# Fourier mixing with a soft mixture of experts: two tiles Z for the turned spectra, and their moves spread over each batch

## The chip, the core and the metric

The kernel runs on one core of a Trainium2 chip. Its engines are called as in the profile: PE (TensorE, matmuls), DVE (VectorE), ACT (ScalarE), POOL (GpSimd) and SP (SyncE, which here issues nearly all DMA transfers). The metric is the time of one execution on the device in microseconds (us), the median of three runs. Lower is better.

## The reference

Eight batches of 2496 tokens with 256 channels go through a Fourier transform along the tokens, a complex linear layer with soft shrinkage, and the transform back; the result is the input of a soft mixture of 8 experts with 4 slots each. Cut to what matters:

```python
X = np.fft.rfft(x, axis=1)                     # x: (8, 2496, 256)
Yr = Xr @ w_r - Xi @ w_i + b_r
Yi = Xr @ w_i + Xi @ w_r + b_i
Y  = sign(Yr) * max(|Yr| - 0.01, 0) + 1j * (the same of Yi)
y  = np.fft.irfft(Y, n=2496, axis=1)           # the tokens of the mixture, N = 19968

logits     = y @ phi                           # (N, 32)
d          = softmax of logits over the tokens
slot_input = d.T @ y                           # (32, 256)
slot_out   = relu(slot_input @ w1[e]) @ w2[e]  # for each expert e and its 4 slots
c          = softmax of logits over the slots
out        = c @ slot_out                      # (N, 256)
```

## The kernel before

The length 2496 is split as 39 x 64, so the transform is done in two steps of small matmuls. The main work runs over 40 steps: 8 batches of 5 groups of 4 frequencies out of 39 (`steps`, line 1071). For each step the program does, by the names that the profile shows:

- `pa`: the first transform (39) of a later batch, on PE; its result goes by way of `ast` to DRAM (`adr`) and comes back turned as `ap`.
- `px`: the second transform (64), on PE from `ap`; ACT, DVE and POOL split its result into high and low parts `xth`, `xtl`, `xsm`, `xsh`, `xsl`.
- `pk` and `py`: the linear layer, on PE from those parts; DVE adds them up to `ut`, and the shrinkage makes `rt` of `ut`, by turns on POOL and on ACT with DVE.
- `tp_p`: the projection on phi. `c_stages`: once a batch, the logits of the batch before go back to tokens. Their coefficients leave for DRAM and come back turned (`gd` written from `g_sb`, then read as `gp`), go through matmuls (`pL`), a maximum (`mx`, transposed on PE as `pm`), exponentials, a second such way through DRAM (`ed`, `eb`), and end as weights `dd` with which `pr` sums up the slots.

`pr` needs the spectra turned, with frequencies on the partitions. For groups 3 and 4 of a batch (and all of the last batch) PE transposes them into tiles `T`. For groups 0 to 2 of batches 0 to 6 (`moved`, line 578) DVE transposes blocks of 32 x 32 into one tile `Z` for each batch (line 669, in the trace `z<-rt`), and sixteen transfers of 96 KB each move these blocks to their partitions in a tile `Y` (`z_move`, line 583, in the trace `y<-z`). There is one tile Z and there are two tiles Y (line 276). A new Z can be written only when all sixteen moves out of the old one have landed.

Order and queues: every operation is a generator step with a due time on a common plan clock, 4 units a step, 20 a batch (a batch takes some 51 us in the trace). A heap hands the steps out in the order of their times, and what is handed out stays in that order on its engine. So an engine, and SP too, does its instructions one behind the other, and one that waits holds up those behind it. SP's transfers take eight semaphores in turn, so a transfer also waits until the eighth before it has landed. `PLAN["zd"]` has the due times of the sixteen moves within their batch: three at 14.9 to 15.9, thirteen at 21.2 to 26.6; in batch 6 the last six come at 28.7 to 30.2 (`z6`).

In the tail the experts' weights are loaded, 32 pieces of 512 KB (`load_w`, line 1116; `wl` lists the due time, the place and the layer of each, counted from the end of the main work, TB = 166). They go to tiles that are free by then: place 't' takes a tile of the pool `ta`, which is opened where the tiles of the first transform lay (`nw`: 13 tiles of 4 KB a partition), 'Y' and 'Z' a third of a tile Y or Z, others what their letters say. The same pool then serves the last stage (`ct`, `chl`: the turned combination weights). From the third group of batch 7 on, the spectra `rt` lie in parts of a tile Z as well (line 648). `hps` is the first product of the experts, `po` the second, `pq` in the last stage the output blocks, written from `ost`.

Of the kernel before, what the change touches and what calls it, by code (L numbers as in the profile page):

```python
# [17 lines left out]
B, N, D = 8, 2496, 256  # L18
N1, N2 = 39, 64
R, G = 3, 22  # L20
# [59 lines left out]
def _constants():  # L80
# [84 lines left out]
PLAN = {  # L165
    "aq": [-10.6, -6.6, -2.6, 1.4, 5.4, 7.4],
    "aqo": [0.4, 0.5],
    "aqt": ["pf", "pt"],
    "eo": {0: [3.95, 1.95], 4: [3.95, 3.9], 5: [2.05, 2.0]},
    "xq": 7.5,  # L170
    "aq2": {(2, 0): [6.6, 8.8, 9.2, 10.4], (2, 1): [8.8, 11.2, 11.6, 13.4]},
    "th": 'PA',
    "sh": 'A',
# [18 lines left out]
    "to": 0.4,  # L192
    "ws": [-29, -28.9, -28.8, 2],
    "late": {'6': {'cms': [13.1, 13.2, 18, 22.65, 22.66, 22.67], 'pd': [16.681, 16.6], 'pdt': ('pl', 'pl'), 'pda': 1, 'pLt': ('ps', 'ps'), 'pr': [17.15, 18.3, 20.179, 19.707, 19.902], 'pL': [6.6, 7.3], 'pm': 8.51, 'pmr': 9.35, 'pb': 10.36, 'pe': [11.747, 11.96, 12.419], 'pg': [0.875, 1.275], 'fr': {'sinv': 0, 'm2': 0, 'f1': 0, 'suni': 0}, 'pbx': 1.2, 'pet': ('pf', 'pf'), 'so': 0.2}, '5': {'so': 1.5}, '4': {}},
    "T_": {'wl': [[-31, 't', 1], [-30, 't', 1], [-29, 't', 1], [-21.8, 't', 2], [-20.6, 't', 2], [-16.9, 't', 1], [-16.8, 't', 1], [-16.6, 't', 2], [-16.1, 't', 2], [-15.6, 't', 2], [-15.1, 't', 2], [-14.6, 't', 2], [-14.1, 't', 2], [-13.6, 'Y', 1], [-13.1, 'Y', 1], [-12.4, 'c', 2], [-11.8, 's', 1], [-11.2, 'a', 1], [-10.6, 'a', 1], [-10, 'a', 1], [-9.5, 'Ww_r', 1], [-8.7, 'Wnws', 1], [-8.6, 'Wwd', 1], [0.01, 'k', 1], [0.01, 'u', 1], [0.02, 'x', 2], [0.02, 'x', 2], [0.02, 'x', 2], [1.4, 'R', 2], [1.4, 'R', 2], [1.73, 'Z', 2], [1.74, 'Z', 2]], 'cl': 2.0, 'cp': 46.5, 'ct': 46.6, 'du': [[2.55, 2]], 'd1': [], 'cm': [19.9, 19.91, 19.92, 25, 25.1, 25.2], 'cm7': [0.71, 1.7, 1.95, 2.7, 2.71, 2.8], 'ye': 0.2, 'te': [[5.6, 0.2], [5.5, 0.4]], 'pg': [-15.49, -11.49, -7.99, -3.934, -2.9], 'yt': 0.578, 'wr': -30.6, 'tp': [0, 0.6, 0.85, 0.5], 'tt': [0.4, 0.55, 0.821, 1.25, 0.994], 'z': 1.686, 'th': [0.1, 0.12], 'tl': [0.24, 0.25], 'pgt': ['ps', 'ps', 'ps', 'pf', 'pf'], 'ch': [0.263, 0.5, 0.7, 1.0, 1.514, 2.0], 'te7': 'AAAAAAAAAA', 'op': 2, 'ot': [3, 5, 7], 'gt': [-14.5, -10.5, -7.0, -3.93, -2.89]},
    "f1": [-1.6, -1.5],
    "kw": [[-28.6, 4], [-28.4, 12]],
    "ap1": 1.85,
    "f0": 0.2,
    "nw": [13, 9],  # L200
    "te": 'A',
    "tp": [0.5, 0.9, 1.9, 1.8],
    "tt": [0.52, 2.505],
# [22 lines left out]
    "hA": 3,  # L226
    "tlr": 1.85,
    "xle": 0.45,
# [32 lines left out]
def fourier_soft_moe_kernel(ctx: ExitStack, tc: tile.TileContext, t: dict, out: bass.AP):  # L261
# [11 lines left out]
    psum_bufs = {"pf": 2, "pl": 2, "pt": 2, "ps": 1, "pr": 1}  # L273
    a_bufs = {"xr": 3, "xh": 3, "xl": 3, "ast": 3}
    main_bufs = {"xsm": 2, "k1": 2, "ut": 2, "rt": 4, "lg": 2}
    chain_bufs = {"ap": 3, "xth": 3, "xtl": 3, "xsh": 3, "xsl": 3, "Z": 1, "Y": 2, "T": 8, "p_sb": 2, "g_sb": 1,
                  "gp": 2, "L": 1, "ee": 1, "g7": 1, "dd": 2, "mx": 1, "dg": 1, "cm": 1, "cs": 1, "ch": 2, "cl": 2,
                  "cb": 1}

# [3 lines left out]
    def wtile(shape, dt, tag, name):  # L283
        if tag in a_bufs:
            return wap.tile(list(shape), dt, tag=tag, name=name, bufs=a_bufs[tag])
        if tag in main_bufs:
            return wmp.tile(list(shape), dt, tag=tag, name=name, bufs=main_bufs[tag])
        return wcp.tile(list(shape), dt, tag=tag, name=name, bufs=chain_bufs[tag])

    parts = {}  # L290

    def part(tag, n, name):

        z, o = parts.get(tag, (None, 12))
        if o + n > 12:
            z, o = wtile([128, 12 * 256], F32, tag, name), 0
        parts[tag] = (z, o + n)
        return z[:, o * 256 : (o + n) * 256]

    x = t["x"]  # L300
# [24 lines left out]
    def sp(**kw):  # L325
        with tc.issue_after(sp_last[-1].ins) if sp_last else nullcontext():
            sp_last.append(tc.keep_in_program_order(nc.sync.dma_start(**kw)))
# [36 lines left out]
    def load_x0():  # L364
        g = GP * len(x0)
        xr = (part("Y", 2, f"x0_{g}") if g >= 8 * GP else wtile([128, GP * D], F32, "T", f"x0_{g}")).rearrange("p (g d) -> p g d", d=D)
        sp(out=xr, in_=x[0, :, g : g + GP, :])
        x0.append(xr[:P1])
# [10 lines left out]
    while len(x0) < G // GP:  # L379
# [6 lines left out]
        wmp.tile([128, n, 64], F32, tag=f"smov{i}", name=f"smov{i}") for i, n in enumerate((KG + 1, K1 + 1 - KG))  # L386
    ]
    wri = part("Z", 4, "wri").rearrange("p (g d) -> p g d", d=D)
    pk0, pk1 = (cons.tile([128, sum(w)], F32, tag=n, name=n) for n, w in PACK.items())
    cols = {}  # L390
    for z, (n, w) in zip((pk0, pk1), PACK.items()):
        o = 0
# [29 lines left out]
    def a_unit(b, g, u):  # L422
# [19 lines left out]
        if g == gs[0]:  # L442
            own = PLAN["ast4"].get((b, g))
            if own == "Z":
                asts[(b, g)] = part("Z", 4, f"ast{b}_{g}")[:QA].rearrange("p (g d) -> p g d", d=D)
            elif own:
                asts[(b, g)] = wtile([QA, 4, D], F32, own, f"ast{b}_{g}")
            else:
                asts[(b, g)] = wtile([QA, 6, D], F32, "ast", f"ast{b}_{g}")
# [132 lines left out]

    def z_move(b):
        for n, (i, j) in enumerate(itertools.product(range(4), range(4))):
            yield 20 * b + (PLAN["zd"][n] if b < B - 2 or n < 10 else PLAN["z6"] + 0.3 * (n - 10))
            if n == 0:
                parts.pop("Y", None)
                yts[b] = wtile([128, 4, 2, KZ, 32], F32, "Y", f"y{b}")
            sp(
                out=yts[b][32 * j : 32 * j + 32, i].rearrange("p h k x -> p (h k x)"),  # L590
                in_=zts[b][32 * i : 32 * i + 32, j].rearrange("p h k x -> p (h k x)"),
            )
# [523 lines left out]
    def load_w(loc, layer):  # L1116
        i = len(wbuf)
        w, h, e = wlist[layer].pop(0)
        if w == 0:
            src = t["moe_w1"][e, h * 128 : h * 128 + 128, :]  # L1120
        else:
            src = t["moe_w2"][e, h * 512 : h * 512 + 512, :].rearrange("(p f) d -> p (f d)", f=4)
        if loc in "YZT":
            parts = [part(loc, 4, f"w{i}")]
        elif loc == "c":
            parts = [wtile([128, F // 4], F32, z, f"w{i}_{z}{q}") for z in ("ch", "cl") for q in range(2)]
        elif loc == "h":
            parts = [wtile([128, F // 4], F32, z, f"w{i}_{z}{q}") for z in ("xsh", "xsl") for q in range(2)]
        elif loc == "a":
            parts = [wtile([128, F], F32, "ap", f"w{i}")]  # L1130
        elif loc == "t":
            parts = [ta_tile(f"w{i}")]
        elif loc == "s":
            parts = [wmp.tile([128, K1 + 1 - KG, 64], F32, tag="smov1", name=f"w{i}").rearrange("p m q -> p (m q)")[:, :F]]
        elif loc[0] == "W":
            parts = [wmp.tile([128, F // 2], F32, tag=loc[1:] + z, name=f"w{i}_{z}") for z in "hl"]
        else:
            tags = {"x": ("xth", "xtl"), "k": ("k1", "k1"), "u": ("ut", "ut"), "R": ("rt", "rt")}[loc]
            parts = [wtile([128, F // 2], F32, tags[q], f"w{i}_{q}") for q in range(2)]
        n = F // len(parts)  # L1140
        for q, r in enumerate(parts):
            sp(out=r, in_=src[:, q * n : q * n + n])
        wbuf[(w, h, e)] = parts
# [4 lines left out]
    def ta_tile(name):  # L1148
        return pools["ta"].tile([128, F], F32, tag="tw", name=name, bufs=NTA)
# [36 lines left out]
    for b in range(B - 1):  # L1186
        step_to(z_move(b))
# [8 lines left out]
    for t_ in PLAN["T_"]["wl"]:  # L1196
        at(t_[0], load_w, *t_[1:])
    at(PLAN["T_"]["z"], slot_stationary)
    T_ = PLAN["T_"]
# [325 lines left out]
```

## Time and profile before

| what | value |
|---|---|
| time, median of 3 runs | 526.41 us (525.14 to 527.59) |
| the profiled execution | 527.98 us, of which the span of its instructions is 526.2 us |
| PE busy | 484.4 us, 92% |
| DVE, ACT, POOL busy | 363.3 us (69%), 319.8 us (61%), 271.0 us (52%) |
| DMA | 131.04 MB, mean 249 GB/s |
| chain of work that ended last | PE 72%, DMA 10%, DVE 8%, issue 3%, POOL 3%, ACT 2% |

The span runs from the first to the last instruction; the profiled execution's time has 1.8 us around it. In the rows of a timeline, the number in square brackets is how long the engine was idle before the instruction, and what by the trace ended that wait; where an instruction waits for several things, this is the one that came last by the profile. Rows of SP are the issue of transfers, not their landing; a row's "x4" is four instructions, and its duration runs from the start of the first to the end of the last.

### The profile page before, as it was taken

How to read it: one execution, taken by the hardware profiler on the slowest of the kernel's cores; microseconds unless marked ns; L12 is line 12 of the kernel's file. 1: busy time of each engine (PE TensorE's matmuls, PEld its weight loads, DVE VectorE, ACT ScalarE, POOL GpSimd, SP SyncE). 2: the span in 40 equal slices, each digit the busy share in tenths (PEclk: the TensorE clock that was granted, in tenths of full speed). 3: DMA queues.
4: the chain of work that ended last, by engine and by line, in shares of the span. 5: the costliest groups of instructions: out<-in, count | busy, mean ns of one | idle time of the engine just before them, and what ended most of it. 6: DMA issues, size and time to landing. Idle time of an engine off the chain costs nothing.

```text
span 526.2 us, 11975 instructions
## 1 busy us (share of the span) xinstructions
PE 484.4 (92%) x4438; PEld 394.7 (75%) x4438; DVE 363.3 (69%) x718; ACT 319.8 (61%) x724; POOL 271.0 (52%) x277
## 2 busy tenths in 40 slices
PE   8889999999979998999899989998997389999991
PEld 4479788878868887888789778888986376468880
DVE  3255975798759966986799589959874186446671
ACT  4357566677656766676577667755754156247771
POOL 0026667767846785678567766844460213214210
PEclk9989999999999999999999999999999599999997
DMA  8998688686877697779677967766586979359998
GB/s 288 323 292 294 218 283 231 191 279 189 253 212 248 174 263 212 243 197 293 185 262 198 287 202 242 189 190 193 173 228 182 355 276 308 110 164 385 405 405 338
DMA packets 90461, 131.04 MB, mean 249 GB/s; under 512 B 40204, under 2 KB 61836, under 8 KB 90404
## 3 DMA queue, kind: packets, MB, share of 16 engines
q1 hardware_dynamic: 89460, 128.16, 75.9%
q10 hardware_dynamic: 944, 2.13, 1.2%
q8 instruction: 35, 0.57, 0.5%
q14 instruction: 22, 0.18, 0.1%
HBM read 69.25 MB, written 50.00 MB: 227 GB/s over the span
## 4 chain that ended last, share of the span: by engine, by line
PE 72%; DMA 10%; DVE 8%; issue 3%; POOL 3%; ACT 2%; SPq 1%; DVEq 0%; ACTq 0%; POOLq 0%
PE py L333 17%; PE px L333 11%; PE pq L333 10%; PE pa L333 8%; PE pk L333 8%; PE pt L708 3%; PE pr L333 3%; DMA w<-in_moe_w 2%; DMA gd<-g_sb 2%; DVE z L257 2%; PE pc L708 2%; PE pe L333 2%; PE pL L333 1%; PE pd L333 1%; DMA xr<-in_x 1%
## 5 line engine op out<-in xcount | busy, mean ns | idle before, releaser
L257 POOL TENSOR_TENSOR xsl<-xsm,xsh 128x256 fp32r<-128x256 f32 x77 | 70.2, 912 | 117.2 <-ACT xsh L257 116.5
L333 PEld LDWEIGHTS px<-smov,ap 128*128 128x128 f32 x640 | 79.8, 194 | 21.4 <-ACT xsh L257 16.1
L333 PE MATMUL px<-smov,ap 128*128 128x128 f32 x640 | 86.2, 279 | 8.9 <-DVE xtl L257 7.8
L257 DVE SCALAR_TENSOR_TENSOR ut<-py,pk,k 128x256 f32<-128x256 f32 x160 | 69.7, 477 | 23.8 <-PE py L333 21.6
L257 ACT COPY ast<-pa 128x512 f32<-128x512 f32 (+1 forms) x88 | 45.5, 560 | 28.5 <-PE pa L333 28.3
L333 PE MATMUL pk<-xsl,w_rh 128*128 128x256 f32 (+1 forms) x160 | 45.4, 283 | 11.6 <-POOL xsl L257 11.6
L257 DVE TENSOR_TENSOR xtl<-px,xth 128x512 fp32r<-128x512 f32 x80 | 54.3, 680 | 0.1
L257 ACT CAST xsh<-xsm 128x256 fp32r<-128x256 f32 x80 | 32.8, 410 | 35.0 <-DVE xsm L257 34.9
L333 PE MATMUL py<-xth,nwsh 128*128 128x256 f32 (+1 forms) x160 | 53.2, 333 | 0.0
L257 ACT CAST xth<-px 128x512 fp32r<-128x512 f32 x80 | 47.2, 591 | 6.1 <-PE py L333 5.1
L257 POOL TENSOR_TENSOR rt<-ut,rt 128x512 f32<-128x512 f32 x36 | 50.8, 1410 | 0.1
L257 DVE TENSOR_TENSOR xsm<-px,xsm 128x256 f32<-128x256 f32 x80 | 33.3, 416 | 23.2 <-ACT xth L257 17.7
L333 PE MATMUL pk<-xsh,w_rh 128*128 128x256 f32 (+1 forms) x160 | 47.9, 299 | 0.0
L257 ACT COPY xsm<-px 128x256 f32<-128x256 f32 x80 | 30.0, 375 | 27.6 <-PE px L333 23.8
L333 PE MATMUL py<-xth,wdh 128*128 128x256 f32 (+1 forms) x160 | 45.2, 283 | 0.0
L333 PE MATMUL py<-xtl,nwsh 128*128 128x256 f32 (+1 forms) x160 | 45.1, 282 | 0.0
L333 PE MATMUL py<-xth,nwsl 128*128 128x256 f32 (+1 forms) x160 | 45.1, 282 | 0.0
L333 PE MATMUL pk<-xsh,w_rl 128*128 128x256 f32 (+1 forms) x160 | 45.0, 281 | 0.0
L333 PE MATMUL py<-xtl,wdh 128*128 128x256 f32 (+1 forms) x160 | 44.9, 281 | 0.0
L333 PE MATMUL py<-xth,wdl 128*128 128x256 f32 (+1 forms) x160 | 44.9, 280 | 0.0
L257 DVE STREAM_TRANSPOSE z<-rt 128x512 f32<-128x512 f32 x42 | 28.2, 694 | 24.1 <-DMA ap<-adr 10.4
L257 DVE SCALAR_TENSOR_TENSOR rt<-ut,rt 128x512 f32<-128x512 f32 x44 | 37.3, 848 | 9.4 <-ACT rt L257 9.4
(227 smaller groups left out, 1304.2 us busy)
## 6 DMA issues: line engine op xcount, KB each, us to landing
ap<-adr SPq DMA_DIRECT2D x76, 256.0 KB
out<-ost SPq DMA_DIRECT2D x37, 512.0 KB
xr<-in_x SPq DMA_DIRECT2D x35, 512.0 KB
adr<-ast SPq DMA_DIRECT2D x20, 768.0 KB
y<-z SPq DMA_DIRECT2D x112, 96.0 KB
w<-in_moe_w SPq DMA_DIRECT2D x21, 512.0 KB
adr<-ast SPq DMA_DIRECT2D x7, 512.0 KB
w<-in_moe_w SPq DMA_DIRECT2D x14, 256.0 KB
```

The costliest lines, as they stand in the source:

```text
L257: return lambda *a, **k: self.tc.keep_in_program_order(f(*a, **k))
L333: tc.keep_in_program_order(nc.tensor.matmul(**kw))
L708: tc.keep_in_program_order(nc.tensor.transpose(out=out, in_=in_, identity=identity))
```

## The change

There are two tiles Z. The sixteen moves of a batch are spaced evenly: every 1.2 plan units from 15.0 to 33.0 of their batch, in batch 6 every 0.6 units from 15.0 to 24.0. To make room, the pool `ta` has ten tiles in place of thirteen; three of the weights get the new place 'z', the thirds of a tile Z of their own (the key "zw" keeps it apart from the Z that `rt` takes parts of). In `wl` the weights at -21.8 and -20.6 are now of the first layer and those at -16.9 and -16.8 of the second; the ones at -14.8 (before -15.1), -14.6 and -14.1 go to 'z'. The line of `wl` itself is left out below.

```diff
-    "nw": [13, 9],
+    "nw": [10, 9],
...
-    "zd": [14.9, 15.4, 15.9, 21.2, 21.65, 22.1, 22.55, 23.0, 23.45, 23.9, 24.35, 24.8, 25.25, 25.7, 26.15, 26.6],
+    "zd": [15.0, 1.2, 0.6],
     "nd": 4,
-    "z6": 28.7,
...
-    chain_bufs = {"ap": 3, "xth": 3, "xtl": 3, "xsh": 3, "xsl": 3, "Z": 1, "Y": 2, "T": 8, "p_sb": 2, "g_sb": 1,
+    chain_bufs = {"ap": 3, "xth": 3, "xtl": 3, "xsh": 3, "xsl": 3, "Z": 2, "Y": 2, "T": 8, "p_sb": 2, "g_sb": 1,
...
-    def part(tag, n, name):
+    def part(tag, n, name, key=None):
 
-        z, o = parts.get(tag, (None, 12))
+        key = key or tag
+        z, o = parts.get(key, (None, 12))
         if o + n > 12:
             z, o = wtile([128, 12 * 256], F32, tag, name), 0
-        parts[tag] = (z, o + n)
+        parts[key] = (z, o + n)
         return z[:, o * 256 : (o + n) * 256]
...
         for n, (i, j) in enumerate(itertools.product(range(4), range(4))):
-            yield 20 * b + (PLAN["zd"][n] if b < B - 2 or n < 10 else PLAN["z6"] + 0.3 * (n - 10))
+            yield 20 * b + PLAN["zd"][0] + PLAN["zd"][1 + b // (B - 2)] * n
...
         if loc in "YZT":
             parts = [part(loc, 4, f"w{i}")]
+        elif loc == "z":
+            parts = [part("Z", 4, f"w{i}", "zw")]
```

The two tiles are taken in turn. Batches 1, 3 and 5 lie in one and 0, 2, 4 and 6 in the other; `rt` of batch 7, asked for next, gets the tile that batch 5 had, the three weights behind it get batch 6's. On PE, DVE, ACT and POOL the instructions stand in the order in which they stood before; only SP's order differs.

First place: SP around the way through `gd`, in batch 2 (the same pattern stands in every batch). `y` from `z` are the moves of batch 2, `c_dr` stores combination weights, `xr` is input, `adr` from `ast` the first transform's result, `ap` its reading back. Before:

```order
L327 DMA c_dr_126<-cb_2491 128x704
L327 DMA y_2297<-z_2030 32x768 x4
L327 DMA xr_4_2722<-in_x 128x1024
L327 DMA y_2297<-z_2030 32x768
L327 DMA adr_1770<-ast_12_2561 128x1536
L327 DMA y_2297<-z_2030 32x768
L327 DMA ap_4_2783<-adr_1029 64x4x256 x2
L327 DMA gd_2858<-g_sb_2735 64x20x32 x2
L327 DMA gp_2883<-gd_2858 40x704 x2
```

and in the changed kernel:

```order
L327 DMA c_dr_126<-cb_2493 128x704
L327 DMA y_2302<-z_2025 32x768 x2
L327 DMA xr_4_2718<-in_x 128x1024
L327 DMA adr_1771<-ast_12_2562 128x1536
L327 DMA ap_4_2777<-adr_1030 64x4x256 x2
L327 DMA y_2302<-z_2025 32x768 x2
L327 DMA gd_2854<-g_sb_2731 64x20x32 x2
L327 DMA gp_2879<-gd_2854 40x704 x2
```

Of the six moves ahead of `gd` two are left ahead of `xr`, and two stand directly ahead of `gd`; four more of the batch's moves stand behind `gp`.

Second place: SP at the end of the main work, behind the last way through `gd` (batch 6). `w` are the weights, `y` from `z` the last moves of batch 6. Before:

```order
L327 DMA gp_5913<-gd_5903 40x640
L327 DMA y_5443<-z_5201 32x768 x2
L327 DMA w_5956<-in_moe_w 128x1024
L327 DMA w_5963<-in_moe_w 128x1024
L327 DMA y_5443<-z_5201 32x768
L327 DMA w_5966<-in_moe_w 128x1024
L327 DMA y_5443<-z_5201 32x768
L327 DMA w_5973<-in_moe_w 128x1024
L327 DMA y_5443<-z_5201 32x768 x2
L327 DMA w_5989<-in_moe_w 128x1024
```

and in the changed kernel, from the last move of batch 6 on:

```order
L327 DMA y_5448<-z_5196 32x768
L327 DMA c_dr_130<-cb_5630 128x704
L327 DMA w_5766<-in_moe_w 128x1024
L327 DMA w_5825<-in_moe_w 128x1024
L327 DMA ap_4_5859<-adr_4156 64x4x256 x2
L327 DMA gd_5909<-g_sb_5841 64x20x32 x2
L327 DMA gp_5919<-gd_5909 40x704 x2
L327 DMA gp_5919<-gd_5909 40x640
L327 DMA w_5960<-in_moe_w 128x1024
L327 DMA w_5967<-in_moe_w 128x1024
L327 DMA w_5969<-in_moe_w 128x1024
```

The six moves that stood among the weights are gone from there; the last move of batch 6 stands ahead of `c_dr` and of the way through `gd`.

## Rows read from the trace of the kernel before

**Rows 1.** The page, part 1: busy time of PE, share of the span, instructions

```profile
PE 484.4 (92%) x4438; PEld 394.7 (75%) x4438; DVE 363.3 (69%) x718; ACT 319.8 (61%) x724; POOL 271.0 (52%) x277
```

**Rows 2.** Stages: length, busy of PE, PEld, DVE, ACT, POOL; clock, DMA share, GB/s

```profile
150.00:201.00 51.00, 48.90 (x484) 41.18 (x484) 40.42 (x80) 34.70 (x79) 35.41 (x34) 1.00 0.75 227
...
404.00:421.00 17.00, 5.59 (x25) 4.67 (x24) 2.56 (x4) 2.77 (x7) 3.72 (x4) 0.60 1.00 341
421.00:452.00 31.00, 29.05 (x404) 21.95 (x403) 22.24 (x55) 17.41 (x45) 7.13 (x10) 1.00 0.82 287
...
415.80:420.00 4.20, 4.19 (x16) 3.69 (x17) 0.51 (x1) 1.25 (x3) 2.07 (x2) 0.50 1.02 407
```

**Rows 3.** Timeline of PE: start, length, instruction, [idle before, what ended it]

```profile
112.50 0.32 PE L831 MATMUL pm<-pk,mx 117*128 117x117 f32 x1 [0.46 <-DVE mx L257]
...
152.07 1.13 PE L333 MATMUL px<-smov,ap 128*128 128x128 f32 x8 [3.13 <-DVE xtl L257]
...
203.20 1.02 PE L333 MATMUL px<-smov,ap 128*128 128x128 f32 x7 [1.83 <-DVE xtl L257]
...
253.91 0.80 PE L333 MATMUL px<-smov,ap 128*128 128x128 f32 x5 [1.43 <-DVE xtl L257]
...
304.59 0.79 PE L333 MATMUL px<-smov,ap 128*128 128x128 f32 x5 [1.38 <-DVE xtl L257]
...
365.88 0.29 PE L831 MATMUL pm<-pk,mx 117*128 117x117 f32 x1 [1.45 <-DVE mx L257]
```

**Rows 4.** Timeline of DVE: transposes into z in batches 1, 2 and 6

```profile
96.74 1.90 DVE L257 STREAM_TRANSPOSE z<-rt 128x512 f32<-128x512 f32 x3 [0.88 <-POOL rt L257]
...
143.78 0.29 DVE L257 TENSOR_TENSOR p_sb<-pq,pk 128x128 f32<-128x128 f32 x1 [0.28 <-PE pq L708]
149.12 1.90 DVE L257 STREAM_TRANSPOSE z<-rt 128x512 f32<-128x512 f32 x3 [5.05 <-DMA gd<-g_sb]
...
352.06 0.71 DVE L257 STREAM_TRANSPOSE z<-rt 128x512 f32<-128x512 f32 x1 [3.03 <-DMA y<-z]
```

**Rows 5.** Timeline of SP: transfers issued around gd

```profile
135.36 1.88 SPq L327 DMA_DIRECT2D y<-z  x3
...
137.91 2.41 SPq L327 DMA_DIRECT2D y<-z  x4
...
141.60 0.53 SPq L327 DMA_DIRECT2D adr<-ast  x1
142.17 0.51 SPq L327 DMA_DIRECT2D y<-z  x1
142.78 2.24 SPq L327 DMA_DIRECT2D ap<-adr  x2
145.57 2.06 SPq L327 DMA_DIRECT2D gd<-g_sb  x2
152.33 1.05 SPq L327 DMA_DIRECT2D gp<-gd  x3
```

**Rows 6.** Timelines of SP, ACT, POOL and PE in the late stretch

```profile
401.24 1.22 SPq L327 DMA_DIRECT2D y<-z  x2
...
407.44 6.17 SPq L327 DMA_DIRECT2D w<-in_moe_w  x6
...
401.55 0.41 ACT L257 CAST xsh<-xsm 128x256 fp32r<-128x256 f32 x1
...
414.46 0.61 POOL L257 TENSOR_SCALAR rt<-ut 128x512 f32<-128x512 f32 x1 [15.69 <-DMA w<-in_moe_w]
...
415.81 0.58 PE L333 MATMUL pk<-xsl,w_rh 128*128 128x256 f32 x1 [11.41 <-POOL xsl L257]
```

**Rows 7.** Timeline of ACT: the copy gp in two batches

```profile
105.14 0.25 ACT L257 COPY gp<-gp 40x64 f32<-40x64 f32 x1 [1.38 <-DMA gp<-gd]
...
156.10 0.25 ACT L257 COPY gp<-gp 40x64 f32<-40x64 f32 x1
```

**Rows 8.** Timeline of PE: the experts' second product begins

```profile
460.26 1.05 PE L333 MATMUL po<-w,z 128*32 128x256 f32 x16
```

More of the change, by code (lines that the diff above doesn't have):

```diff
@@ L194 @@
     "late": {'6': {'cms': [13.1, 13.2, 18, 22.65, 22.66, 22.67], 'pd': [16.681, 16.6], 'pdt': ('pl', 'pl'), 'pda': 1, 'pLt': ('ps', 'ps'), 'pr': [17.15, 18.3, 20.179, 19.707, 19.902], 'pL': [6.6, 7.3], 'pm': 8.51, 'pmr': 9.35, 'pb': 10.36, 'pe': [11.747, 11.96, 12.419], 'pg': [0.875, 1.275], 'fr': {'sinv': 0, 'm2': 0, 'f1': 0, 'suni': 0}, 'pbx': 1.2, 'pet': ('pf', 'pf'), 'so': 0.2}, '5': {'so': 1.5}, '4': {}},
-    "T_": {'wl': [[-31, 't', 1], [-30, 't', 1], [-29, 't', 1], [-21.8, 't', 2], [-20.6, 't', 2], [-16.9, 't', 1], [-16.8, 't', 1], [-16.6, 't', 2], [-16.1, 't', 2], [-15.6, 't', 2], [-15.1, 't', 2], [-14.6, 't', 2], [-14.1, 't', 2], [-13.6, 'Y', 1], [-13.1, 'Y', 1], [-12.4, 'c', 2], [-11.8, 's', 1], [-11.2, 'a', 1], [-10.6, 'a', 1], [-10, 'a', 1], [-9.5, 'Ww_r', 1], [-8.7, 'Wnws', 1], [-8.6, 'Wwd', 1], [0.01, 'k', 1], [0.01, 'u', 1], [0.02, 'x', 2], [0.02, 'x', 2], [0.02, 'x', 2], [1.4, 'R', 2], [1.4, 'R', 2], [1.73, 'Z', 2], [1.74, 'Z', 2]], 'cl': 2.0, 'cp': 46.5, 'ct': 46.6, 'du': [[2.55, 2]], 'd1': [], 'cm': [19.9, 19.91, 19.92, 25, 25.1, 25.2], 'cm7': [0.71, 1.7, 1.95, 2.7, 2.71, 2.8], 'ye': 0.2, 'te': [[5.6, 0.2], [5.5, 0.4]], 'pg': [-15.49, -11.49, -7.99, -3.934, -2.9], 'yt': 0.578, 'wr': -30.6, 'tp': [0, 0.6, 0.85, 0.5], 'tt': [0.4, 0.55, 0.821, 1.25, 0.994], 'z': 1.686, 'th': [0.1, 0.12], 'tl': [0.24, 0.25], 'pgt': ['ps', 'ps', 'ps', 'pf', 'pf'], 'ch': [0.263, 0.5, 0.7, 1.0, 1.514, 2.0], 'te7': 'AAAAAAAAAA', 'op': 2, 'ot': [3, 5, 7], 'gt': [-14.5, -10.5, -7.0, -3.93, -2.89]},
@@ new lines @@
+    "T_": {'wl': [[-31, 't', 1], [-30, 't', 1], [-29, 't', 1], [-21.8, 't', 1], [-20.6, 't', 1], [-16.9, 't', 2], [-16.8, 't', 2], [-16.6, 't', 2], [-16.1, 't', 2], [-15.6, 't', 2], [-14.8, 'z', 2], [-14.6, 'z', 2], [-14.1, 'z', 2], [-13.6, 'Y', 1], [-13.1, 'Y', 1], [-12.4, 'c', 2], [-11.8, 's', 1], [-11.2, 'a', 1], [-10.6, 'a', 1], [-10, 'a', 1], [-9.5, 'Ww_r', 1], [-8.7, 'Wnws', 1], [-8.6, 'Wwd', 1], [0.01, 'k', 1], [0.01, 'u', 1], [0.02, 'x', 2], [0.02, 'x', 2], [0.02, 'x', 2], [1.4, 'R', 2], [1.4, 'R', 2], [1.73, 'Z', 2], [1.74, 'Z', 2]], 'cl': 2.0, 'cp': 46.5, 'ct': 46.6, 'du': [[2.55, 2]], 'd1': [], 'cm': [19.9, 19.91, 19.92, 25, 25.1, 25.2], 'cm7': [0.71, 1.7, 1.95, 2.7, 2.71, 2.8], 'ye': 0.2, 'te': [[5.6, 0.2], [5.5, 0.4]], 'pg': [-15.49, -11.49, -7.99, -3.934, -2.9], 'yt': 0.578, 'wr': -30.6, 'tp': [0, 0.6, 0.85, 0.5], 'tt': [0.4, 0.55, 0.821, 1.25, 0.994], 'z': 1.686, 'th': [0.1, 0.12], 'tl': [0.24, 0.25], 'pgt': ['ps', 'ps', 'ps', 'pf', 'pf'], 'ch': [0.263, 0.5, 0.7, 1.0, 1.514, 2.0], 'te7': 'AAAAAAAAAA', 'op': 2, 'ot': [3, 5, 7], 'gt': [-14.5, -10.5, -7.0, -3.93, -2.89]},
```

## The prediction

> **What bounds the kernel now.** I read the page first: TensorE (PE) is busy for 484.4 us, 92% of the span [rows 1], so at most some 42 us can be won without taking work from it. The table of stages tells where these lie. In a batch of the steady part PE is busy for 48.90 of 51 us; in the stretch from 404 to 421 it is busy for 5.59 of 17 [rows 2]. The first question is who ends those idle times.
>
> In the steady part PE stops once a batch, always ahead of a px: 3.13, 1.83, 1.43 and 1.38 us, each time for DVE's xtl [rows 3]. DVE shows why xtl is late: behind p_sb at 143.78 it stands idle for 5.05 us, then come the transposes into Z [rows 4], and only behind them xtl, for which px waits [rows 3]. The trace puts that wait down to whatever transfer landed last, but a transpose into z needs nothing from gd or ap; what it needs is that all sixteen moves y<-z of the batch before have left the one tile Z. The DMA queue (SP) shows how late these are: from 135.36 on it issues one transfer behind the other, four moves take 2.41 us (0.6 each), and the last stands behind adr, at 142.17 [rows 5]. DVE is let go at 149.12, some 7 us behind its issue.
>
> In the late stretch PE waits 11.41 us for xsl, and POOL, which makes xsl, waits 15.69 us ahead of rt [rows 6]. From batch 7's third group on rt lies in Z, so it needs the moves of batch 6. Six of them, the first two at 401.24, are issued among weights of 512 KB each, and six more weights follow from 407.44 on [rows 6]. PE's clock is at the lower of its two levels (1.2 of 2.4 GHz) when it comes back: granted 0.50 from 415.8 to 420.0 [rows 2], behind that idle time.
>
> **The change part by part.** I sum against the profiled execution, 527.98 us (span 526.2); the median of the three runs, 526.41, lies 1.57 below, and I carry the gain over to it.
>
> *Two tiles Z, steady part.* A transpose now waits for the moves of two batches ago. The last of them is planned at 33.0 of its own batch, the transposes that need the tile some 15 plan units later (a batch is 20 units and 51 us, so about 40 us); the wait for the tile goes whole. That is 3.13 + 1.83 + 1.43 + 1.38 = 7.77 us of PE. What is late next: in batch 1, where the moves were out in time, the same transposes waited 0.88 us for POOL's rt [rows 4], and no px waited behind them; PE lost only 0.46 at pm [rows 3]. Today px comes 1.05 us behind the last of the three transposes (152.07 against 149.12 + 1.90). If DVE starts them 0.9 us behind 144.07, px could start at 147.9, and PE gets there at 148.94. So I count 7.2: 7.77 less about 0.15 a place. Bounds: 7.77, and nothing (first rival).
>
> *Two tiles Z, batch 6.* DVE's wait of 3.03 us at 349 to 352 [rows 4] costs PE no px, since other work stands there, but it pushes the reduction mx, for which PE's pm waits 1.45 us [rows 3]. DVE wins up to 3 us, but mx hangs on the read of gp too; I count 1.0 (bounds 0 and 1.45).
>
> *Late stretch.* rt takes the tile of batch 5's Z, whose moves are out a batch earlier, and the weights "z" take batch 6's, allocated behind rt. The six late moves are gone from among the weights. Nothing else holds POOL: its xsl waits for ACT's xsh, done by 401.96, so with rt's first operation (0.61) and a short one of its own it is ready near 403, and PE gets there at 404.40 [rows 6]. I count 11.0 of 11.41 (bounds 0, third rival, and 11.41).
>
> *Clock.* Waits of up to 3.13 us left it at 1.00 in 150 to 201 [rows 2]; if PE doesn't idle for 11 us, I take it that it stays. The 4.19 us of PE's work between 415.8 and 420.0 at 0.50 [rows 2] takes half at the upper level: 2.1 us (bounds 0 and 2.1).
>
> *Moves spread.* As many moves, as many bytes. The stretch on SP from c_dr to gd holds 6 moves in the kernel before and 4 in the changed one, and two of the four stand directly ahead of gd: 1.2 us of SP's time there. Before, ap is out at 145.02 and gd, which waits for ACT, at 145.57 [rows 5]; with two to four moves fewer ahead of xr, adr and ap these go 1.2 to 2.4 us earlier (none of them waits long in the trace), and the two moves end before gd can go. So gd starts as now, behind an emptier queue, and I count 0. If that cover is missing, it is 1.2 us a batch and more: the first rival. On ACT, POOL, DVE and PE no instruction moves.
>
> *Ten tail buffers, three weights in Z.* The same 32 weights in the same order of layers. The tiles that follow them in the tail come around sooner, but each takes one that was last read many output blocks before (ct6144, wanted near block 36, takes that of blocks 0 to 7). 0; the last stage is 56 us of writing results, which this leaves alone. The three weights wait on SP for batch 6's moves, which stand ahead of the round trip gd, and behind them queue only other weights. 0.
>
> Sum: 7.2 + 1.0 + 11.0 + 2.1 = 21.3. Profiled: 527.98 - 21.3 = 506.7; median: 526.41 - 21.3 = 505.1.
>
> **The rivals.** *The round trip through gd takes the tile's place (0.13).* ACT's copy gp stands in its queue ahead of the casts and evictions that feed PE. In batch 1, without the tile's wait, ACT idled 1.38 us there and PE lost next to nothing; in the batch after, ACT came 3.13 us later by PE's stall and started gp at 156.10 with no wait [rows 7]. Take the stall away and leave gd as late as now, with two moves ahead of it, and ACT waits 3.13 + 1.2 = 4.3 us, 2.9 more than batch 1 bore: the 3.13 are given back. That all steady gains go this way gives 21.3 - 8.2 = 13.1, so 513.3. For it: gd took from 145.57 to 152.33 to let gp go [rows 5]. Against it: that was behind xr, adr and ap, which now start earlier. The Trainium skill (Perfetto Trace Analysis, What "DMA-bound" means) says that where the issuing sequencer's track is solid with DMA slices, descriptor generation is the bound and larger descriptors are what matters. By that rule sixteen moves spread out are as slow as sixteen in a row, and this rival's 513.3 it is; the trace agrees from 135.36 to 145.02 and disagrees behind, where SP issues nothing from 147.63 to 152.33.
>
> *Weights late (0.07).* 27 of 32 weights are issued behind gp, 14.2 MB. The stall gave their transfers time: 341 GB/s in 404 to 421, 287 in 421 to 452 [rows 2]. From 401, they need 41.5 us at the one rate and 49.3 at the other: there by 442.5 or 450.5. The second layer's product po starts at 460.26 [rows 8], 13.1 us earlier then (11.0 + 2.1): 447.2. At the slower rate it waits up to 3.3 us: 508.4; at the faster one not. The 287 held while many loads waited for their tiles, so I take the faster. The Trainium skill (DMA: Bandwidth & Descriptors, Bandwidth, Measured) gives 138 GB/s for a transfer of 64 KB and 341 for 1 MB; an estimate between them for 512 KB, 290, would make this rival's 508.4 likely. The trace shows 407 GB/s in 415.8 to 420.0, with these very pieces in flight.
>
> *The late stall is the weights' own (0.05).* The trace names "DMA w<-in_moe_w" as what released POOL. If rt hung on those, the stall and the clock stay: 21.3 - 13.1 = 8.2, 518.2. Against it: rt reads no weight, and the last moves are out just ahead of six weights, into DMA engines that are full (1.00 in 404 to 421).
>
> *Slower than before (0.02).* One mechanism: gd later still. Besides the 8.2, the round trip would have to cost PE the 13.1 us as well, over six batches 2.2 us each beyond the 1.2 of two moves: gd 3.4 us later than now, near six moves of 0.6 ahead of it. The order has two. From there on the time is 526.4 and more.
>
> **How the numbers follow.** The forecast has 0.73 and lies, with the bounds of its terms (every gain whole 21.3 + 1.4 = 22.7; pm nothing, 1.5 us lost at small new waits, 18.8) and half a per cent of measurement on the far side, in 502 to 508. About 0.5% of the time is what a measurement of this kernel can tell from no change. The range 501.0 to 512.5 takes in late weights and most of the ways in which only a part of the steady gain comes; left out are the full first rival, the late stall that stays, and the slow end, somewhat under 0.2. Faster by over 0.5% (under 523.8): all cases but the last, less 0.02 for what I don't see, 0.96; within 0.5%: 0.02; slower: 0.02.
>
> **What would show it.** In the trace after: DVE's transposes into z with no wait for a transfer, at most some 0.9 us for rt; px without a gap once a batch; PE's busy time of 51 us near 50; ACT's idle time ahead of gp under 1.5 us (above 2.5 it is the first rival); in the late stretch no gap of PE ahead of pk, POOL's rt directly behind its ut, and the granted clock at 1.00 throughout; the weights' loads without a pause and po without a wait for them. Wrong I am if px waits as before (the tile isn't what held it), or if the late gap stays with a weight as its end.

## The result, and the profile after

The changed kernel takes 505.08 us (median of four runs, 503.90 to 506.13) against 525.77 of the kernel before (four runs, 525.12 to 527.59): a ratio of 0.960, interval 0.957 to 0.964. The profiled execution took 503.9 us, its span is 502.1. The forecast was 505.1 in a range of 501.0 to 512.5. Ratios compare fast executions alone; slower ones (two of the eight with twelve moves ahead of `gd`, one of the kernel before) count only in the medians given.

The page of the profile after, part 1, answers [rows 1]: PE's work is the same 4438 matmuls, in a span 24.1 us shorter.

```profile
PE 479.7 (96%) x4438; PEld 390.4 (78%) x4438; DVE 363.5 (72%) x718; ACT 318.1 (63%) x724; POOL 267.6 (53%) x277
```

The table of stages after (columns as in [rows 2]). What follows the late stall lies 24 us earlier, so the row 397 to 428 answers 421 to 452 there. What stands ahead of the stall lies 11 us earlier: the `pk` that came behind it at 415.81 now comes at 393.29, inside the row 380 to 397:

```profile
150.00:201.00 51.00, 50.97 (x500) 42.92 (x501) 41.87 (x83) 35.59 (x83) 36.06 (x36) 1.00 0.82 240
...
380.00:397.00 17.00, 16.76 (x182) 14.51 (x177) 8.80 (x21) 8.81 (x23) 5.71 (x8) 1.00 0.75 233
397.00:428.00 31.00, 29.03 (x406) 22.00 (x404) 22.16 (x55) 17.39 (x45) 7.60 (x11) 1.00 1.04 394
```

In the steady part PE is now busy for 50.97 of 51 us, and where it had worked 5.59 of 17 us around the stall it now works 16.76 of 17, at a granted clock of 1.00.

Why it was idle there is best seen in one row of the groups by line and engine (DVE's transposes into Z: count, busy us and mean ns, then the idle time ahead of them and what the trace says ended it), first of the kernel before, then of the one after:

```profile
L257 DVE STREAM_TRANSPOSE z<-rt 128x512 f32<-128x512 f32 x42 | 28.2, 694 | 24.1 <-DMA ap<-adr 10.4 <-POOL rt L257 5.6 <-DMA gd<-g_sb 5.0
```

```profile
L256 DVE STREAM_TRANSPOSE z<-rt 128x512 f32<-128x512 f32 x42 | 28.1, 692 | 7.9 <-POOL rt L256 7.4 <-DMA ap<-adr 0.5
```

Of 24.1 us of waiting (DVE's, and equal to the difference of the two spans only by chance) 16.2 are gone, and what is left is POOL's `rt`, which the prediction named as next in line. The trace had put the old wait down to `ap` and `gd`, which a transpose doesn't read.

In the timelines after, no `px` of the main work has a wait any more. `pm` still waits twice for `mx`: in batch 1 as before, in batch 6 for 0.96 us in place of 1.45 [rows 3]. Timeline of PE (start, length, instruction, [idle, what ended it]):

```profile
110.24 0.32 PE L831 MATMUL pm<-pk,mx 117*128 117x117 f32 x1 [0.44 <-DVE mx L256]
...
354.93 0.29 PE L831 MATMUL pm<-pk,mx 117*128 117x117 f32 x1 [0.96 <-DVE mx L256]
...
393.29 0.28 PE L333 MATMUL pk<-xsl,w_rh 128*128 128x256 f32 x1
...
436.06 1.05 PE L333 MATMUL po<-w,z 128*32 128x256 f32 x16
```

The `pk` at 393.29 answers the one that came after 11.41 us of idle time [rows 6]. POOL's `rt` ahead of it, which had waited 15.69 us, waits 0.61 for `ut`; its `xsl` then waits for ACT's `xsh`:

```profile
388.43 0.61 POOL L256 TENSOR_SCALAR rt<-ut 128x512 f32<-128x512 f32 x1 [0.61 <-DVE ut L256]
391.10 0.74 POOL L256 TENSOR_TENSOR xsl<-xsm,xsh 128x256 fp32r<-128x256 f32 x1 [2.05 <-ACT xsh L256]
```

To see where the 24.1 us came from I take DVE's `zacc`, which comes once a batch behind PE's `pz`, as a milestone; there are eight. The first, the sixth and the eighth, before:

```profile
140.78 0.16 DVE L257 COPY zacc<-pz 128x1 f32<-128x1 f32 x1 [1.80 <-PE pz L333]
...
391.61 0.21 DVE L257 SCALAR_TENSOR_TENSOR zacc<-zacc,fo,pz 128x1 f32<-128x1 f32 x1 [1.81 <-PE pz L333]
450.44 0.21 DVE L257 SCALAR_TENSOR_TENSOR zacc<-zacc,fo,pz 128x1 f32<-128x1 f32 x1 [1.22 <-PE pz L333]
```

and after:

```profile
138.52 0.16 DVE L256 COPY zacc<-pz 128x1 f32<-128x1 f32 x1 [1.80 <-PE pz L333]
...
380.66 0.21 DVE L256 SCALAR_TENSOR_TENSOR zacc<-zacc,fo,pz 128x1 f32<-128x1 f32 x1 [1.81 <-PE pz L333]
426.24 0.21 DVE L256 SCALAR_TENSOR_TENSOR zacc<-zacc,fo,pz 128x1 f32<-128x1 f32 x1 [1.22 <-PE pz L333]
```

The same three milestones cut every kernel of this study into four stretches. Their lengths, in one profiled execution of each kernel, in us:

| kernel | start to first `zacc` | main work, to the sixth | late stretch, to the eighth | rest of the span |
|---|---|---|---|---|
| before | 140.78 | 250.83 | 58.83 | 75.8 |
| changed | 138.52 | 242.14 | 45.58 | 75.9 |
| tiles alone | 140.14 | 241.86 | 45.23 | 75.8 |
| batch 6 early, one tile | 138.44 | 250.38 | 45.62 | 75.7 |
| all moves early, one tile | 141.16 | 241.46 | 45.96 | 75.8 |
| moves even, one tile | 139.37 | 243.44 | 45.83 | 75.5 |
| warm gap | 138.23 | 252.45 | 56.82 | 76.3 |
| six ahead of `gd` | 140.87 | 242.52 | 45.12 | 75.8 |
| twelve ahead of `gd` | 144.49 | 250.39 | 45.91 | 76.0 |
| warm start and `mx` first | 138.92 | 241.29 | 45.18 | 75.6 |

Between before and changed that is 8.69 us in the main work, 13.25 in the late stretch, nothing in the rest, and 2.26 at the start. The last has nothing to do with the change: the profiled execution of before ran at a granted clock of 0.50 from 34.3 to 41.1, and that of after at 1.00. Two kernels of the table that do the same as before up to there, batch 6 early and the warm gap, took 138.4 and 138.2. How much of the 2.26 is the clock's stays open, since in the first of these two the clock was low as well, from 34 to 38 (0.63 and 0.52 in two stretches of 2 us). (The 144.49 of twelve moves ahead of `gd` is another matter: ACT waits 6.16 us for `gp` in its batch 1.)

### The profile page after: what moved, and what is told of

It is laid out like the page before. It is cut to its first block, busy times and chain, and to the rows that moved or that the text cites. A ratio compares the mean times of both kernels' runs of the same rounds, so it can differ in the third digit from the quotient of the medians.

```text
span 502.1 us, 11977 instructions
## 1 busy us (share of the span) xinstructions
PE 479.7 (96%) x4438; PEld 390.4 (78%) x4438; DVE 363.5 (72%) x718; ACT 318.1 (63%) x724; POOL 267.6 (53%) x277
## 3 DMA queue, kind: packets, MB, share of 16 engines
q10 hardware_dynamic: 944, 2.13, 1.3%
## 4 chain that ended last, share of the span: by engine, by line
PE 73%; DMA 12%; DVE 4%; ACT 2%; POOL 2%; issue 2%; SPq 2%; ACTq 0%; POOLq 0%; DVEq 0%
PE py L333 17%; PE px L333 11%; PE pq L333 10%; PE pk L333 8%; PE pa L333 8%; PE pt L708 4%; PE pr L333 3%; DMA gd<-g_sb 2%; DMA xr<-in_x 2%; PE pc L708 2%; PE pe L333 2%; SPq L327 2%; PE pd L333 2%; DMA w_ch<-in_moe_w 2%; DMA w<-in_moe_w 1%
## 5 line engine op out<-in xcount | busy, mean ns | idle before, releaser
L256 POOL TENSOR_TENSOR xsl<-xsm,xsh 128x256 fp32r<-128x256 f32 x77 | 67.2, 873 | 114.5 <-ACT xsh L256 113.8
L256 POOL TENSOR_TENSOR xl<-xr 128x512 f32<-128x512 f32 (+1 forms) x36 | 43.6, 1210 | 0.0
L256 POOL TENSOR_TENSOR xh<-xr 128x512 f32<-128x512 f32 (+1 forms) x36 | 42.8, 1188 | 0.3 <-DMA xr<-in_x 0.3
```

What stands on the lines that cost most here:

```text
L256: return lambda *a, **k: self.tc.keep_in_program_order(f(*a, **k))
```

## The experiments

All are compared with the kernel before on the same chip, in the same hours; its median was 523.3 us beside tiles alone, batch 6 early, all moves early and the warm gap, 524.0 beside the two with moves ahead of `gd` and the warm start, and 525.0 beside the even moves. So ratios are given.

**Two tiles, the old times of the moves.** The changed kernel with

```diff
-    "zd": [15.0, 1.2, 0.6],
+    "zd": [14.9, 15.4, 15.9, 21.2, ..., 26.6],
+    "z6": 28.7,
...
-            yield 20 * b + PLAN["zd"][0] + PLAN["zd"][1 + b // (B - 2)] * n
+            yield 20 * b + (PLAN["zd"][n] if b < B - 2 or n < 10 else PLAN["z6"] + 0.3 * (n - 10))
```

> The changed kernel with the moves at their old times (six of batch 6 among the weights again): two tiles without the spread. Theory (the tile is what DVE and POOL waited for): the four waits of px and the wait of rt in the late stretch go as in the changed kernel, about 505 us, and DVE's transposes start behind rt of POOL. First rival (the round trip through gd takes the place, since six moves stand ahead of gd again): ACT waits 3 to 4.5 us ahead of the copy gp in batches 2 to 5 and PE gives back 1.4 to 3.1 us each, 508 to 513. Spread needed: over 515.

Measured: 504.11 us, ratio 0.964 (0.957 to 0.971), the same as the whole change. DVE's waits ahead of its transposes into Z are POOL's alone (the row of the groups, as above):

```profile
L257 DVE STREAM_TRANSPOSE z<-rt 128x512 f32<-128x512 f32 x42 | 28.1, 693 | 7.9 <-POOL rt L257 7.9
```

Six moves stand ahead of `gd` again and six more among the weights, and neither costs anything: `gd` goes out at 144.94 (4.80 us behind the first `zacc`, against 4.79 in the changed kernel), ACT waits at most 2.27 us ahead of the copy `gp`, and POOL's `rt` of the late stretch waits 0.62 us for DVE's `ut`. The theory holds, and the spread isn't needed where there are two tiles.

**One tile, batch 6 early.** The kernel before with

```diff
-            yield 20 * b + (PLAN["zd"][n] if b < B - 2 or n < 10 else PLAN["z6"] + 0.3 * (n - 10))
+            yield 20 * b + (PLAN["zd"][n] if b < B - 2 else 15.0 + 0.6 * n)
```

> The kernel before, one tile, with nothing changed but the times of batch 6's sixteen moves (every 0.6 units from 15.0 to 24.0). Theory (rt waited for the last moves out of the one tile): the gap of 11.4 us and the half clock go, the waits of px in batches 2 to 5 stay: 526.4 - 13.1 = 513.3. If the stall is the weights' own (third rival): 525 to 527, gap still there.

Measured: 511.25 us, ratio 0.977 (0.970 to 0.983). The late stretch shrinks to 45.62 us, all of the 13.25 that the change brought, with the same weights in the same places of memory. So the third rival falls: the stall was the last moves', not the weights', though the trace names "DMA w<-in_moe_w" [rows 6]. The waits of `px` stay, and one of them shows a cost that the prediction hadn't counted. DVE, PE, and the stretch of 198.7 to 201.3 (columns as in [rows 2]):

```profile
195.76 1.90 DVE L257 STREAM_TRANSPOSE z<-rt 128x512 f32<-128x512 f32 x3 [4.73 <-DMA ap<-adr]
```

```profile
198.71 2.04 PE L333 MATMUL px<-smov,ap 128*128 128x128 f32 x8 [2.82 <-DVE xtl L257]
```

```profile
198.70:201.30 2.60, 2.59 (x12) 2.60 (x13) 1.86 (x4) 1.05 (x3) 2.60 (x3) 0.50 0.14 42
```

Behind a wait of 2.82 us the granted clock is 0.50 (1.2 GHz) for 2.6 us, which costs some 1.3 us more by its length (half of the 2.6 us).

**One tile, all moves early.** The kernel before with

```diff
-            yield 20 * b + (PLAN["zd"][n] if b < B - 2 or n < 10 else PLAN["z6"] + 0.3 * (n - 10))
+            yield 20 * b + 15.0 + 0.6 * n
```

> The kernel before, one tile, with the moves of every batch every 0.6 units from 15.0 to 24.0. The last move is due 2.6 units (some 6.6 us) earlier than in the kernel before, the longest wait of px was 3.1 us. If the lateness of the moves is the whole cause, one tile does what two do: about 505 us, no px wait. If SP cannot issue them by then beside the rest of its queue, or gd is pushed back, waits of 1 to 3 us a batch stay: 508 to 513. If it is the number of tiles alone: 513 (late stretch only).

Measured: 505.11 us, ratio 0.965 (0.959 to 0.971): one line of code, one tile Z, thirteen tail buffers, and the time of the changed kernel. SP, then DVE's first transposes, in the batch whose rows stand above:

```profile
185.55 1.89 SPq L327 DMA_DIRECT2D y<-z  x3
187.54 0.53 SPq L327 DMA_DIRECT2D c_dr<-cb  x1
...
195.19 1.47 SPq L327 DMA_DIRECT2D gd<-g_sb  x2
```

```profile
194.19 1.90 DVE L257 STREAM_TRANSPOSE z<-rt 128x512 f32<-128x512 f32 x3 [0.50 <-POOL rt L257]
```

The last move is out at 187.44, DVE comes to its transposes at 193.69 and waits for POOL alone. So it is the lateness of the moves that costs, and either cure will do: to move them earlier, or not to need them. For a DMA-bound kernel in which the issuing engine's track is solid with DMA slices, the Trainium skill (Perfetto Trace Analysis, What "DMA-bound" means) asks for large descriptors. SP's track is solid for some 10 of the 51 us of a batch (135.36 to 145.02 before [rows 5]), and here the same sixteen transfers, issued earlier, were enough: DVE's wait in this batch is 0.50 us, against 4.73 in the kernel with batch 6 early, whose steady moves have the old times.

**One tile, moves even, same end.** The kernel before with

```diff
-            yield 20 * b + (PLAN["zd"][n] if b < B - 2 or n < 10 else PLAN["z6"] + 0.3 * (n - 10))
+            yield 20 * b + 15.0 + (0.773 if b < B - 2 else 0.6) * n
```

> The kernel before, one tile, with the sixteen moves of batches 0 to 5 evenly from 15.0 to 26.6 (every 0.773 units: the last is due when the last was due before), batch 6's from 15.0 to 24.0. Even spacing alone, without the earlier end of e3_one_tile_early. If the due time of the last move decides: the waits of px stay at 1.4 to 3 us a batch, 510 to 513, as in e2_batch6_early. If it was the crowd that held the last move back (from 135.36 on SP issued twelve transfers and more without a pause, 0.6 us each, and the last move lay 7 us from its landing): DVE's wait falls under the 2 us that PE does not feel, 505 to 507. The first is the theory as the prediction has it; I hold the second for about as likely.

Measured: 506.43 us, ratio 0.965 (0.962 to 0.967). The second answer: the last move is due when it was due before, but SP, with less of a crowd ahead of it, issues it earlier. SP in the same batch, first of the kernel with batch 6 early, whose steady moves have the old times, then of this one:

```profile
190.28 0.51 SPq L327 DMA_DIRECT2D y<-z  x1
190.89 2.64 SPq L327 DMA_DIRECT2D ap<-adr  x2
```

```profile
187.67 0.51 SPq L327 DMA_DIRECT2D y<-z  x1
188.28 2.64 SPq L327 DMA_DIRECT2D ap<-adr  x2
```

That is 2.6 us by the two traces, and 3.5 against each one's first `zacc`. DVE's wait falls from 4.73 to 2.35:

```profile
194.27 1.90 DVE L257 STREAM_TRANSPOSE z<-rt 128x512 f32<-128x512 f32 x3 [2.35 <-DMA ap<-adr]
...
244.47 1.90 DVE L257 STREAM_TRANSPOSE z<-rt 128x512 f32<-128x512 f32 x3 [2.82 <-DMA y<-z]
```

```profile
247.42 1.13 PE L333 MATMUL px<-smov,ap 128*128 128x128 f32 x8 [0.91 <-DVE xtl L257]
```

DVE still waits 2.3 to 2.8 us in three batches, and PE feels only 0.4 to 0.9 of it. The pairs give a rule for this place: 5.05 and 3.13 before [rows 3, 4], 4.73 and 2.82, 2.82 and 0.91. PE's loss is DVE's wait less 1.9 us each time, in all fourteen pairs of the four kernels with one tile and waits of `px`; at waits of 1.08 and 1.93 us of DVE PE has none.

**The price of the clock.** The kernel before with

```diff
-    "kw": [[-28.6, 4], [-28.4, 12]],
+    "kw": [[-28.6, 4], [-28.4, 12], [152.34, 48]],
```

> The kernel before with 48 matmuls of 128x512 that nobody reads (some 10.2 us at full clock) ahead of the linear layer of batch 7's fourth group, that is, in the gap of 11.4 us. It changes no wait; it prices the clock alone. Theory (the low clock at 415.8 to 420.0 comes from the idle time ahead of it): granted clock 1.00 up to the tail, the gap still ends where POOL's xsl comes, and what follows is 2.1 us earlier: about 524.3. If the low clock has another cause or costs nothing here: 526.4. If the matmuls hold something up: over 527.

Measured: 522.83 us, ratio 0.999 (0.996 to 1.003). In the total that settles nothing, since the 2.1 us looked for are 0.4%. The stretch itself does. PE, and the 4.2 us behind the gap (before they ran at 0.50, [rows 2]):

```profile
402.29 11.18 PE L333 MATMUL wps<-warm 128*128 128x512 f32 x48
...
414.82 0.39 PE L333 MATMUL pk<-xsl,w_rh 128*128 128x256 f32 x1 [0.41 <-POOL xsl L257]
```

```profile
415.00:419.20 4.20, 4.20 (x31) 3.77 (x32) 1.70 (x4) 1.75 (x5) 2.70 (x3) 1.00 1.03 410
```

The stall is still there, but the late stretch is 56.82 us, 2.01 shorter than before, where 2.1 had been counted. That is one execution of each. In this one most of the gain was lost again elsewhere: its main work took 252.45 us, 1.62 more than before, and in it the clock fell behind a wait of `px`.

```profile
148.41 1.22 PE L333 MATMUL px<-smov,ap 128*128 128x128 f32 x8 [2.02 <-DVE xtl L257]
```

```profile
149.20:153.00 3.80, 3.80 (x42) 2.65 (x40) 2.09 (x5) 0.96 (x2) 2.07 (x3) 0.55 0.84 264
```

**Six, then twelve moves ahead of `gd`.** The changed kernel with, for batches 0 to 5,

```diff
-            yield 20 * b + PLAN["zd"][0] + PLAN["zd"][1 + b // (B - 2)] * n
+            yield 20 * b + (15.0 + 1.2 * n if n < 10 else 28.15 + 0.003 * n) ...
```

and with `n < 4` in place of `n < 10`; batch 6 keeps its times.

> The changed kernel with the last six moves of each of the batches 0 to 5 directly ahead of gd (the changed kernel has two there and four behind gp). In the trace of the changed kernel SP stands idle for 3.5 us ahead of gd (139.81 to 143.31), waiting for ACT's g_sb; four more moves of 0.6 us are 2.4 us and fit. Theory: gd no later, about 505 us. First rival as it was priced (each move ahead of gd is that much later at gp): PE gives back 1 to 2 us a batch, 510 to 515.

> The changed kernel with twelve of the sixteen moves of each of the batches 0 to 5 directly ahead of gd. Twelve moves take 7.2 us, two of them and the idle time of SP are 4.7 us: gd goes 2.5 to 4 us later (more if SP has to wait for the landing of earlier ones). ACT has waited up to 2.6 us ahead of gp without PE losing anything, so about half of it comes through: 1 to 3 us of PE in each of five batches, 510 to 520. If the way through gd has no part in what bounds PE: 505. This is the dose from which the first rival would have decided.

Measured: six 505.26 us, ratio 0.965 (0.960 to 0.971); twelve 520.85, ratio 0.992 (0.988 to 0.996). SP with six, then with twelve, in one batch:

```profile
140.97 4.47 SPq L327 DMA_DIRECT2D y<-z  x6
145.67 1.45 SPq L327 DMA_DIRECT2D gd<-g_sb  x2
```

```profile
144.50 8.25 SPq L327 DMA_DIRECT2D y<-z  x12
152.84 1.45 SPq L327 DMA_DIRECT2D gd<-g_sb  x2
```

Six fit into SP's idle time ahead of `gd`; twelve don't, and then the first rival's mechanism runs as the prediction described it. ACT, and PE behind it, in the next batch:

```profile
211.57 0.24 ACT L256 COPY gp<-gp 40x64 f32<-40x64 f32 x1 [4.36 <-DMA gp<-gd]
```

```profile
212.26 0.43 PE L333 MATMUL pL<-chpL,m2h 120*128 120x352 f32 x1 [0.95 <-ACT chpL L256]
218.17 0.32 PE L831 MATMUL pm<-pk,mx 117*128 117x117 f32 x1 [0.62 <-DVE mx L256]
```

A batch takes 51.3 us (195.18 to 246.45 between two `zacc`) against 49.2 in the changed kernel, 1.6 of it in these two waits, and the main work is 8.25 us longer: the whole steady gain is gone. But it needed ACT waits of about 4 us (3.39 to 4.46). With six, ACT waits up to 2.4 us and the main work is 0.4 us longer than in the changed kernel.

**Warm start, and `mx` first.** The changed kernel with

```diff
-    "kw": [[-28.6, 4], [-28.4, 12]],
+    "kw": [[-28.6, 4], [-28.4, 12], [2.99, 4]],
...
-            yield t0 + PLAN["tlo"] + PLAN["zo"][2 * (grp > 0) + e]
+            yield t0 + PLAN["tlo"] + PLAN["zo"][2 * (grp > 0) + e] + (0.45 if (b, grp, e) in PLAN["zl"] else 0)
```

where `zl` holds the second half of group 2 in batches 1 and 6.

> The changed kernel with two small edits that the runs suggest: four matmuls of 128x512 that nobody reads ahead of the first transform's unit at which PE waits near 32 us (behind that wait the granted clock is 0.50 for some 4 us in four of the six traces), and in batches 1 and 6 the last transpose into Z behind DVE's reduction mx instead of ahead of it (0.70 us of the 0.96 and 0.44 that pm waits). If both hold: up to 2 us in the executions with the low clock at the start and some 1.0 us in all: 503 to 504. If the start's low clock comes anyway: 504 to 505. If the matmuls delay the start more than they save: 505 to 506.

Measured: 504.05 us over six runs, ratio 0.962 (0.958 to 0.966): not told apart from the change. In its profile the wait of `pm` in batch 6 is gone (that of batch 1 is not, 0.45), and PE waits 0.65 us for `chpe` a little later instead; the main work is 0.85 us shorter. Whether the start's low clock is prevented, six runs don't show (this execution didn't have it, and some without the edit don't either).

```profile
360.20 0.42 PE L334 MATMUL pe<-chpe,f1h 117*120 117x352 f32 x1 [0.65 <-ACT chpe L257]
```

## Why the prediction was right

Step by step, against the milestones:

- **Two tiles Z, steady part:** counted 7.2 us, measured 8.02 between the first and the fifth milestone (they lie 52.42, 51.12, 50.73 and 50.69 us apart before, and 49.2 each after). The reading was right: the transposes waited for the moves out of the one tile, and behind them stood `xtl`. The 0.15 a place taken off for a new wait wasn't there: DVE now waits 0.50 us for POOL's `rt`, and up to 1.9 us PE feels nothing, as the pairs above show. The waits went whole, 7.77 us, and the slower first `px` behind each (1.13 us in place of 1.06) makes up the rest.
- **What the prediction couldn't tell:** which of the two parts brings that. It gave the tile all and the spread nothing. The runs show that the tiles alone bring it (241.86 us of main work), and that one tile does too when its moves end early enough (241.46 with the last due at 24.0). So 0 for other times of the moves is right only with the second tile in place. The changed kernel's own times, with the last move due at 33.0, were not run with one tile.
- **Batch 6, `pm`:** counted 1.0, measured 0.67 (391.61 - 345.74 = 45.87 before, 45.20 after). The size was off because `mx` hangs on `gp` as much as on the transposes: ACT waits 2.13 us for it there after the change, 0.89 before. In five of the kernels without the old stall of the transposes (changed, tiles alone, all moves early, moves even, six ahead of `gd`) the wait of `pm` is that of ACT less 1.16 to 1.19 us. The prediction had named `gp`, and gave it too little.
- **Late stretch and clock:** counted 11.0 and 2.1, measured 13.25 together. That the row of POOL named the weights as what ended the wait was rightly set aside; one tile with batch 6's moves early brings the same. The clock's share is 2.0 us by the stretch that was kept warm, which leaves 11.2 for the wait.
- **Moves past `gd`:** counted at 0 for the reason that SP would be waiting for ACT ahead of `gd` anyway. In the trace after, SP is through with the two moves at 139.81 and issues `gd` at 143.31:

```profile
138.56 1.25 SPq L327 DMA_DIRECT2D y<-z  x2
143.31 1.45 SPq L327 DMA_DIRECT2D gd<-g_sb  x2
147.48 1.05 SPq L327 DMA_DIRECT2D gp<-gd  x3
```

- **The first rival** failed at its premise, and not at its price. It took the way through `gd` to be as long as before; from the issue of `gd` to that of `gp` it is 4.17 us in the rows above, against 6.76 before [rows 5], and ACT waits 0.44 to 1.63 us in batches 2 to 5, not 4.3. What ACT bears without loss at `pL` is more than the 1.38 us that batch 1 had shown [rows 7]: with twelve moves ahead of `gd` PE loses 0.95 there behind an ACT wait of 4.36, so some 3.4 us are free at that place. But `pm` then loses 0.62 more, and the batch is 2.0 us longer; with waits of this size the whole steady gain went, as the rival had said. One of the prediction's signs was missed: ACT's wait ahead of `gp` was to stay under 1.5 us, with the first rival above 2.5. It is 1.63 in batch 4, where PE loses nothing, 2.13 in batch 6, where `pm` waits its 0.96, and 2.61 in batch 7, where `pL` follows without a wait for ACT. So 1.5 was too tight a bound for "no loss", and 2.5 no sure sign of the rival.
- **Ten buffers, three weights in Z:** counted 0. The rest of the span behind the last milestone is 75.8 us before, 75.9 after, and 75.5 to 76.3 with either set of buffers.
- **Weights:** `po` starts at 436.06 without a wait. The stretch of 397 to 428 moves 394 GB/s in all, against 287 in its counterpart before [rows 2], so the faster of the two rates in the second rival (341) was the nearer one, and still too low. The estimate of 290 from the Trainium skill's two figures (DMA: Bandwidth & Descriptors, Bandwidth, Measured) is contradicted by this row. (The slower rate's 450.5 in the prediction should be 450.3, 401 + 49.3; nothing hangs on it.)

The counted terms add up to 21.3, and the measured ones (8.02, 0.67, 13.25) to 21.9. That the median came out at 505.08 beside 505.1 is in part luck, since it is closer than the terms were: the steady part was 0.8 too small, `pm` 0.3 too large, the medians differ by 20.7 us, and the profiles by 24.1, with the start's 2.26 in it.

## What to carry to other kernels

Where an engine waits ahead of writing into a tile, look for the slowest reader of what lay in that tile, and not at the transfer that the trace names; the name is only that of what landed last. Before a second buffer is paid for with memory, see whether the old buffer's readers can go earlier: here earlier times of sixteen small transfers alone did the same. And a wait costs what it exceeds the slack behind it (1.9 us between DVE's transposes and `px`, 3.4 between ACT's `gp` and `pL`), which two executions with different waits give by a subtraction; what other places behind it lose, as `pm` did, comes on top.

## What the runs showed of the hardware

- Waits of PE far shorter than the 11 us of the late stretch can be followed by the lower clock: 0.50 for 2.6 us behind a wait of 2.82, and 0.55 for 3.8 us behind one of 2.02, while in the kernel before a wait of 3.13 left it at 1.00 [rows 2, 3]. So a wait may cost more than its length, and not in every execution.
- Twelve transfers of 96 KB in a row take 8.25 us of SP, 0.69 each, and six take 4.47, 0.75 each: a little more than the 0.6 of four in a row [rows 5]. The median of a single issue is 0.59 us in all three kernels, so the excess lies in a few longer ones (the longest 1.6) or between them.
